# Block-sparse attention with Fourier mixing on one core: folded Fourier stage, exp in place in PSUM, two-unit slots, queues in written order

## The chip, the cores and the metric

The kernel runs on one core of a Trainium2 chip. The metric is the device time of one execution in microseconds (us), lower is better. The profile shows five queues of the core that run side by side (in the 229.0 us of batch 0's attention before, PE was busy 143.5 us, DVE 215.5, POOL 191.6 and ACT 79.6): PE (matrix products, with weight loads shown apart as PEld), DVE, ACT and POOL (element-wise work), and SP, which here only issues transfers. PEclk in the profile is the clock that was granted to PE, 1.00 being full speed; the traces record either 1.00 or 0.50 at any one time, and other values are means. All timed and profiled runs compared here were fast-state runs.

## The reference

The input is a batch of 4, with 8 heads, 768 tokens and head size 64. Attention is followed by a Fourier mixing layer and two dense layers:

```
attn = exp(scores * scale), masked by 32x32 blocks, rows normalised;   o = attn @ v
x    = o with the heads side by side                       # 4 x 768 x 512
u    = x + real(fft(fft(x, tokens), channels))
un   = (u - mean(u)) / sqrt(var(u) + 1e-6)
out  = u + relu(un @ w_ch1) @ w_ch2                        # 512 -> 2048 -> 512
```

## The kernel before

Attention works in *units*: a pair of heads, half of the queries (384 columns), 128 keys. There are 12 units in a pair of heads, 4 pairs in a batch and 192 units in all. One unit goes PE (scores), ACT (exp), DVE (mask), PE (values), while POOL adds the masked exponentials for the row sums:

```
        s = ps_s.tile([P, 2, 512], FP32, tag="s", name="s")     # PSUM, two buffers
        ... two score matmuls into s ...
        e = ep.tile([P, 2, HS], FP32, tag="e", name="e")        # SBUF
        nc.scalar.activation(out=e, in_=s[:, :, 0:HS], func=ACT.Exp, scale=scale)
        m = mask[:, c, half * HS:(half + 1) * HS].rearrange("p (o s) -> p o s", o=1)
        nc.vector.tensor_tensor(out=e, in0=e, in1=m.broadcast_to([P, 2, HS]), op=ALU.mult)
        ...
        nc.gpsimd.tensor_add(out=acc_of[n, half], in0=acc_of[n, half], in1=e)
```

The Fourier stage is done with cosine and sine tables on PE, along tokens and then across channels, using one symmetry (half the output columns). Once per pair a *turn* transposes q and k of the next pair. During batch 0 the two weight matrices are also rounded, in 16 pieces, on ACT, DVE and POOL. The main loop:

```
    for u in range(units + 9):
        if u < units:            scores(u)          # with exp, mask and sums
        if 0 <= u - 3 < units:   values(u - 3)
        ...  place, norm, mix, turn, and every third u: w_round(u // 3)
```

The order of this text is only a wish: the framework's scheduler decides how the instructions stand in each queue.

## Time and profile before

| quantity, from the trace before | value |
|---|---|
| device time, median | 1554.4 us |
| busy: PE / DVE / POOL / ACT | 1369 / 674 / 465 / 271 us |
| start of the first normalising multiply | 259.5 us |
| one later pair of heads | 34.3 us |
| Fourier stage, first normalising multiply (618.3) to first hidden matmul (678.9) | 60.6 us |
| period of a batch | 358.5 us |

PE is the busiest engine, but it isn't full everywhere: attention leaves it idle (27.7 of 34.3 us busy in a later pair) and batch 0 is filled by DVE and POOL (215.5 and 191.6 of 229.0 us). A saving on an engine therefore counts only in a stage where that engine is what the others wait for.

### The profile page before, as it was taken

The numbers are of one execution on the slowest core, as the hardware profiler recorded it, in microseconds if no ns is written. First come the engines' busy times: TensorE is split into PE (matmuls) and PEld (weight loads), VectorE is DVE, ScalarE is ACT, GpSimd is POOL, SyncE is SP. The second block draws the span as 40 slices with busy tenths as digits, with TensorE's granted clock in tenths as the row PEclk, the third lists the DMA queues.
The fourth block names the chain that finished last, engine by engine and source line by source line (L and its number), as shares of the span: only waits on it lengthen the run. The fifth ranks groups of instructions, "written<-read, shape, count | busy, mean of one in ns | idle before, by whom it ended". The sixth has DMA issues, their size and how long they took to land.

```text
span 1551.9 us, 11529 instructions
## 1 busy us (share of the span) xinstructions
PE 1369.0 (88%) x4657; PEld 678.0 (44%) x4657; DVE 673.6 (43%) x682; ACT 271.1 (17%) x383; POOL 465.1 (30%) x253
## 2 busy tenths in 40 slices
PE   6664478999999887999999888999999887999998
PEld 3111123764553222675454222485454322685453
DVE  3999997320003878240001788440000777240000
ACT  3343322100001333000000333101000323000000
POOL 2898885000002666010000666210000558010000
PEclk9777788999999998999999999999999989999999
DMA  7323210000001111000001111000000200000000
GB/s 257 102 92 118 85 29 24 0 0 7 14 7 42 33 31 31 1 0 7 14 1 41 31 35 37 0 1 0 19 2 14 53 16 1 0 1 0 21 0 22
DMA packets 63008, 46.19 MB, mean 30 GB/s; under 512 B 51404, under 2 KB 56548, under 8 KB 61668
## 3 DMA queue, kind: packets, MB, share of 16 engines
q1 hardware_dynamic: 61604, 41.97, 9.1%
q10 hardware_dynamic: 1344, 3.42, 0.6%
q8 instruction: 38, 0.62, 0.2%
q14 instruction: 22, 0.18, 0.0%
HBM read 39.08 MB, written 6.29 MB: 29 GB/s over the span
## 4 chain that ended last, share of the span: by engine, by line
issue 36%; PE 32%; DVE 25%; POOL 5%; ACT 2%; DMA 1%; SPq 0%; POOLq 0%; DVEq 0%; ACTq 0%
DVE e L269 18%; PE z L345 8%; PE pq L361 6%; PE hp L401 5%; PE y L417 5%; POOL acc L272 3%; PE s L263 2%; PE o L286 2%; DVE w_sb L218 2%; DVE wraw L216 1%; ACT e L267 1%; PE m L173 1%; PE sp L306 1%; DVE x L333 1%; DVE wraw L221 1%
## 5 line engine op out<-in xcount | busy, mean ns | idle before, releaser
L269 DVE TENSOR_TENSOR e<-e,mask 128x768 f32<-128x768 f32 x192 | 356.9, 1903 | 75.0 <-ACT e L267 75.0
L417 PE MATMUL y<-w_sb,hs 128*128 128x512 f32 x768 | 333.8, 593 | 0.0
L401 PE MATMUL hp<-unT,w_sb 128*128 128x384 f32 x1024 | 332.5, 486 | 0.0
L274 POOL TENSOR_TENSOR acc<-acc,e 128x768 f32<-128x768 f32 x128 | 290.7, 2271 | 10.4 <-DVE e L269 1.0
L263 PE MATMUL s<-qT,kT 64*128 64x384 f32 x768 | 213.6, 596 | 46.2 <-ACT e L267 46.2
L401 PEld LDWEIGHTS hp<-unT,w_sb 128*128 128x128 f32 x1024 | 194.2, 190 | 136.8 <-issue 4.8
L272 POOL TENSOR_TENSOR acc<-e 128x768 f32<-128x768 f32 x32 | 63.7, 1991 | 633.6 <-PE sp L306 632.0
L286 PE MATMUL o<-e,vr 128*64 128x384 f32 x768 | 186.6, 561 | 44.6 <-DVE e L269 41.7
L417 PEld LDWEIGHTS y<-w_sb,hs 128*128 128x128 f32 x768 | 145.1, 190 | 177.6 <-issue 172.2
L267 ACT ACTIVATE e<-s 128x768 f32<-128x768 f32 x192 | 152.0, 809 | 360.3 <-POOL acc L272 153.3
L419 DVE TENSOR_TENSOR x<-y,x 128x512 f32<-128x512 f32 x24 | 16.6, 691 | 321.3 <-PE y L417 321.3
L409 DVE TENSOR_SCALAR hs<-hp 128x768 f32<-128x768 f32 x32 | 30.6, 957 | 284.7 <-PE hp L401 284.7
L263 PEld LDWEIGHTS s<-qT,kT 64*128 64x128 f32 x768 | 69.4, 205 | 158.0 <-ACT e L267 74.0
L286 PEld LDWEIGHTS o<-e,vr 128*64 128x64 f32 x768 | 41.8, 146 | 172.1 <-DVE e L269 87.1
L407 ACT ACTIVATE hs<-hp 128x768 f32<-128x768 f32 x32 | 25.9, 810 | 444.4 <-PE hp L401 444.4
L345 PE MATMUL z<-cs_sb,x 128*128 128x385 f32 x192 | 76.1, 548 | 11.7 <-DVE x L333 11.7
L243 PE MATMUL tp<-ident,kr 128*128 128x128 f32 x96 | 21.6, 349 | 57.4 <-DVE qT L246 42.1
L374 POOL TENSOR_SCALAR rstd<-mv 128x1 f32<-128x1 f32 x24 | 5.2, 217 | 222.7 <-DVE mv L372 222.7
L345 PE MATMUL z<-sn_sb,x 128*128 128x385 f32 x192 | 64.8, 486 | 0.0
L345 PEld LDWEIGHTS z<-cs_sb,x 128*128 128x128 f32 x192 | 40.3, 215 | 45.5 <-issue 16.7
L223 POOL TENSOR_TENSOR wraw<-wraw 128x1024 f32<-128x1024 f32 x16 | 46.0, 2876 | 46.1 <-DVE wraw L221 21.6
L349 DVE COPY zs<-z 128x385 f32<-128x385 f32 x16 | 9.0, 560 | 107.6 <-ACT zc L348 107.6
(78 smaller groups left out, 832.1 us busy)
## 6 DMA issues: line engine op xcount, KB each, us to landing
wraw<-in_moe_w_ch_dram SPq DMA_DIRECT2D x16, 1024.0 KB, 5.0
qr<-in_q_dram SPq DMA_DIRECT2D x32, 192.0 KB, 3.5
kr<-in_k_dram SPq DMA_DIRECT2D x32, 192.0 KB, 3.3
vr<-in_v_dram SPq DMA_DIRECT2D x32, 192.0 KB, 2.5
out_dram<-x SPq DMA_DIRECT2D x24, 256.0 KB, 2.0
cs_sb<-in_cos_s_dram ACTq DMA_DIRECT2D x1, 1155.0 KB, 5.3
sn_sb<-in_sin_s_dram ACTq DMA_DIRECT2D x1, 1155.0 KB, 7.8
cd_sb<-in_cos_d_dram ACTq DMA_DIRECT2D x1, 514.0 KB, 5.4
```

What stands on the lines that cost most here:

```text
L218: nc.vector.scalar_tensor_tensor(out=dst.bitcast(U32), in0=hi, scalar=0x80000000, in1=a, op0=ALU.bitwise_and, op1=ALU.bitwise_or)
L223: nc.gpsimd.tensor_mul(out=a.bitcast(FP32), in0=lo.bitcast(FP32), in1=a.bitcast(FP32))
L263: nc.tensor.matmul(s[:, i, 0:HS], kT[D * i:D * i + D, c * P:(c + 1) * P], qT[D * i:D * i + D, half * HS:(half + 1) * HS], start=True, stop ...
L267: nc.scalar.activation(out=e, in_=s[:, :, 0:HS], func=ACT.Exp, scale=scale)
L269: nc.vector.tensor_tensor(out=e, in0=e, in1=m.broadcast_to([P, 2, HS]), op=ALU.mult)
L272: nc.gpsimd.tensor_add(out=acc_of[n, half], in0=e_of[u - 1], in1=e)
L274: nc.gpsimd.tensor_add(out=acc_of[n, half], in0=acc_of[n, half], in1=e)
L286: nc.tensor.matmul(o[D * i:D * i + D, :], vt[:, i, c, :], e[:, i, :], start=(c == 0), stop=(c == C - 1))
L345: nc.tensor.matmul(z[:, g, 0:KS], x[:, c, d * P:(d + 1) * P], tab[:, c, :], start=(c == 0), stop=(c == C - 1))
L361: nc.tensor.matmul(pq[:, g, 0:KD], zz[:, d, c:S:C], tab[:, d, :], start=(d == 0), stop=(d == ND - 1))
L401: nc.tensor.matmul(ps[:, j, 0:G * P], w1_sb[:, d, f * P:(f + 1) * P], unT[g][:, d, :], start=(d == 0), stop=(d == ND - 1))
L417: nc.tensor.matmul(y, hs[f // (NF // 2)][:, f % (NF // 2), o * P:(o + 1) * P], w2_sb[:, f, :], start=(f == 0), stop=(f == NF - 1))
```

## The change

The intent was threefold: less PE work in the Fourier stage (both symmetries folded away on DVE first, tokens in an order that pairs them), a cheap mask multiply, and a known order of work. Cut to its core (reordered; cuts are marked):

```
-        e = ep.tile([P, 2, HS], FP32, tag="e", name="e")
-        nc.scalar.activation(out=e, in_=s[:, :, 0:HS], func=ACT.Exp, scale=scale)
+        nc.scalar.activation(out=s[:, :, 0:HS], in_=s[:, :, 0:HS], func=ACT.Exp, scale=scale)
+        e = ep.tile([P, 2, HS], FP32, tag="e", name="e")
-        nc.vector.tensor_tensor(out=e, in0=e, in1=m.broadcast_to([P, 2, HS]), op=ALU.mult)
+        nc.vector.tensor_tensor(out=e, in0=s[:, :, 0:HS], in1=m.broadcast_to([P, 2, HS]),
+                                op=ALU.mult)
 ...
-    acc_p: 1 buffer;  ps_t: 2 (PSUM);  ps_o: 2
+    acc_p: 2 buffers; ps_t: 1 (PSUM);  ps_o: 1;  ps_m: 2, for the Fourier and dense layers
-    WN = 1024          # weight rounding in 16 pieces
+    WN = 512           # in 32 pieces
 ...
+        def fold():    # sums and differences of mirrored tokens and channels, on DVE
+            tt(out=sa, in0=xA, in1=xB, op=ALU.add)
+            tt(out=sd, in0=xA, in1=xB, op=ALU.subtract)
+            ... 14 operations; then about a quarter of the matmuls, then unfolding on DVE
 ...
+    def slot(sl):                                  # two units
+        if sl > 0 and sl <= B * SB:
+            for u in units:
+                values(u - SLOT)
+        if sl < B * SB:
+            for u, s in [(u, scores(u)) for u in units]:
+                weigh(u, s)                        # exp, mask, sums
+        ... place, row sums; at the third slot after a batch: norm, Fourier, dense layers
+        if sl % SP == 3 and sl // SP + 1 < len(pairs):
+            turn(sl // SP + 1)
+        ... v load; from slot 4 on: one table copy
+        while w_next < min(len(wchunks), 2 * sl):
+            w_round(w_next)
+            w_next += 1
+    with tc.manual_schedule():                     # queues keep the order of the text
+        for sl in range(B * SB + 6):
+            slot(sl)
```

A switch that hands out the dense layers in pieces among the attention slots is in the code, but off. Not shown: the mask's numbers go from BF16 to 8-bit integers, the Fourier tables are now put in order by copies during batch 0, and a check on the size of q and k moves from DVE to ACT, where it is part of the turn.

## The prediction

> **What bounds the kernel now.** I read the page first: its chain, then the slices.
>
> ```profile
> issue 36%; PE 32%; DVE 25%; POOL 5%; ACT 2%; DMA 1%; SPq 0%; POOLq 0%; DVEq 0%; ACTq 0%
> ...
> PE   6664478999999887999999888999999887999998
> ...
> DVE  3999997320003878240001788440000777240000
> ```
>
> No single engine bounds it. Four batches repeat one pattern: attention (DVE digits 7 to 9), the Fourier stage, then two dense matmul layers (PE 9, DVE 0). "Issue 36%" is PE streaming through those layers. So I cut the span into stages (start:end, length, busy us per engine, granted PE clock, DMA):
>
> ```profile
> 34.00:263.00 229.00, 143.49 (x549) 47.23 (x548) 215.52 (x136) 79.64 (x100) 191.55 (x75) 0.79 0.26 80
> 263.00:323.00 60.00, 59.50 (x220) 44.37 (x220) 25.09 (x57) 5.20 (x11) 4.76 (x13) 0.96 0.00 1
> 323.00:494.00 171.00, 171.00 (x485) 86.83 (x483) 15.63 (x20) 11.20 (x16) 0.00 (x0) 1.00 0.04 14
> 510.00:545.00 35.00, 27.88 (x122) 9.50 (x122) 26.73 (x20) 11.66 (x18) 22.22 (x11) 0.90 0.14 34
> ```
>
> The columns after the length are PE, PEld, DVE, ACT, POOL. Batch 0 attention also rounds the weights and is bound by DVE (94%) with POOL behind it. Fourier and dense layers are bound by PE. One later head pair takes 34.3 us (equal chain pieces start at 545.10 and 579.40) with no engine full: a round of waits. The batch period is 358.5 us (first Fourier matmul after 263.7, 622.4, 980.8). Two groups and two waits say what the round is:
>
> ```profile
> L269 DVE TENSOR_TENSOR e<-e,mask 128x768 f32<-128x768 f32 x192 | 356.9, 1903 | 75.0 <-ACT e L267 75.0
> L274 POOL TENSOR_TENSOR acc<-acc,e 128x768 f32<-128x768 f32 x128 | 290.7, 2271 | 10.4 <-DVE e L269 1.0
> ...
> POOL acc L272 <- PE sp L306: 632.0, 26, 171.3
> ...
> ACT e L267 <- POOL acc L272: 153.3, 32, 8.4
> ```
>
> The single accumulator keeps POOL waiting for PE's row sums, and exp waits for POOL to give back an e buffer. And the mask multiply is slow only beside POOL:
>
> ```profile
> 610.88 0.55 DVE L312 TENSOR_TENSOR sums<-sp,sums 128x384 f32<-128x384 f32 x1
> ...
> 613.62 4.32 DVE L269 TENSOR_TENSOR e<-e,mask 128x768 f32<-128x768 f32 x2 [1.73 <-ACT e L267]
> ...
> 624.68 1.81 DVE L269 TENSOR_TENSOR e<-e,mask 128x768 f32<-128x768 f32 x2
> ...
> 612.82 8.98 POOL L274 TENSOR_TENSOR acc<-acc,e 128x768 f32<-128x768 f32 x4
> ```
>
> POOL's adds end at 621.8. Two multiplies before that take 4.32 us, two after it 1.81. L312, whose first operand is in PSUM, takes 0.55 us although a POOL add runs from 610.93.
>
> [...] L269 (two SBUF inputs) 0.945 us alone, a median of 2.56 fully beside POOL; L312 (one) the same either way; a POOL add 1.80 alone, 2.41 beside L269. [...] the clock record drops to half for 6.8 us once per pair, hence 0.90. [...] each of these drops follows the turning of q and k.
>
> **The change, part by part.** The new program leaves its interleaving switch off, so each queue runs as written: two-unit slots (24 per batch), and at the third slot after a batch its norm, Fourier stage and dense layers, with no attention inside.
>
> *Attention slot.* From the trace: one unit's scores occupy PE 0.84 us and are complete after 0.92; exp starts 0.11 later and takes 0.81; DVE follows after 0.03; values take 0.80 and start 0.05 after the multiply. The multiply from PSUM I take as 0.96 (fit: PSUM operations of 384 and 512 elements took 0.55 and 0.69), next start 0.08 before its end. As PE is in order (values, values, scores, scores), the loop is 0.80 + 0.92 + 0.11 + 0.81 + 0.03 + 0.88 + 0.96 + 0.05 = 4.56 us per two units. POOL needs 1.67 x 1.8 = 3.0, so its waits vanish.
>
> *Turn slot, one in six.* With one transpose buffer (two before), x's transposes and four groups of q and k alternate with copies: after the second multiply (3.70) the x copy ends at 4.2, then four rounds of about 0.55 (three transposes) + 0.55 (copy) + 0.15 of hand-over, the last copy hidden: values begin at 8.2, the slot takes 9.8. PE idles or only transposes for 6 us, so the 6.8 us drop of the clock stays; values and scores at half clock took 1.48 and 1.58, twice the time, which delays the chain by some 2.8.
> Pair: 5 x 4.56 + 9.8 + 2.8 = 35.4 us against 34.3. The much cheaper multiply gains nothing here: its time comes back as exposed PE chain. Per slot 5.9.
>
> *Batch 0.* 32 half-size roundings, two in each of 16 slots. POOL: 2 x 2.9 (half of 2.88 + 2.80, plus overhead) + 1.67 x 2.1 = 9.3; DVE: 2 x 2.85 (half of 2.44 + 2.04 + 1.06, plus overhead) + 2 x 0.88 + 1 for copies and tables = 8.5. They hinder each other: 9.5 per slot. Start 35 (34.1 before) + first slot 5 + 16 x 9.5 + 9 x 5.9 + 4 = 249 at the first norm (258 before, with 56 units done instead of 54).
>
> *Fourier.* Before: norm at 618.1, first hidden matmul at 681.5: 63.4, all on PE but the first 4. PE's new work: 5,769 columns along tokens and 2,309 across; a 384-column matmul costs 0.645, so 9.7 and 3.9 us instead of 32.7 and 21.5. But DVE works alone around it. Norm: two multiplies beside POOL (1.81, 2.21) and four of 0.60 = 6.4. Fold: SBUF-SBUF at 1.04 ns per element (0.68 for 512, 0.945 for 768), 14 operations, PE released after 7.3. Along: 9.7, plus 2.5 for a cold clock. First across matmuls, copy out: 1.6. Then per 128 tokens on DVE: two of 0.46, eight of about 0.20 and two tiny ones, statistics 0.73 + 0.18, rstd wait 1.0, normalize 0.46 = 5.1; three, plus 1.1 for the odd row: 16.4. Last transposes and copy 1.2. Sum 45.1, and 2.5 for the cold start of the hidden layer: 47.6. Gain 16 per batch.
>
> *Dense layers.* Unchanged matmuls: 165.5 (last batch, 1379.4 to 1544.9) + 1.3 for transposes = 167. In the 171.3 of the earlier batches some attention and twelve transposes were tucked in; now they are exposed, and that is in the slots.
>
> *Sum.* One batch adds 47.6 + 167 = 215 to its slots. 249 + 4 x 215 + 70 remaining slots x 5.9 - 4 + 12 for the tail (three nearly empty slots, and the 7 us that lie between the last matmul and the end before) = 1530 span; the device time is 2 to 3 above that. As I counted every wait in full, I settle at 1525.
>
> **The rivals.** (a) *Attention really becomes faster*: if the clock doesn't drop and the transposes interleave better, a pair takes 31 instead of 35.4: 79 slots are 13 pairs, 57 us less, about 1468. For it: PE stays busy in 3.3 of 4.56 us; against: the drop came with every turn before. (b) *Old order was worth more*: the old schedule slipped attention into the dense layers and placed work wherever an engine was free; strictly ordered queues may add waits that I don't see (24 small q loads per pair at about 0.6 us of issue each are 14 us of 35, hidden if loaded a pair ahead). 1 us more per slot is 1600. For it: DVE, ACT and PE are now tied in one loop; against: the loads are a pair ahead. (c) *PE work sets it*: the 45 us saved per batch on PE came fully through: 4 x 45 = 180 less, 1375. Against: PE waits for fold and for across on DVE, in program order, with nothing else to do.
>
> **Range and chances.** The slot is the weight: 0.3 us on 70 slots is 21; 5 us on a Fourier stage is 20; batch 0 is sure to 12. Together about 32: 1465 to 1575 holds it 8 in 10, wider than the sum because in-order waits add up one way. The 2% line (1524) lies at my estimate: faster 0.47, same 0.43, slower 0.10.
>
> **What would show it.** Right: the multiply near 0.96 us and POOL's add near 1.8 outside batch 0; pairs of 34 to 36 us; granted clock still near 0.9 there; Fourier stage 45 to 50 us with PE busy under half of it and DVE waited for; dense layers 167. Wrong: a multiply from PSUM still over 1.3 us; a pair under 32 or over 38; DMA or SP among the long waits; batch 0's norm before 235 or after 270.

Passages that no trace of this case shows are cut from the paragraph on the mask multiply and the clock, and a clause from the expectation of experiment 12; the cuts are marked. The sum came to a span of 1530 us, from which the prediction settled at 1525. What it says of the clock and of PE's order, with the numbers beside it:

- Half clock: in the later batches of the kernel before, in each of the eight turns with a stretch of 4.6 us in which PE idles or only transposes, a drop of 6.8 us begins within that stretch; the three turns tucked into the dense layers (longest such stretch 0.7 us) show none, so of these eleven "every turn" holds for the eight alone. That the drop stays in the new turn slot is inferred from this.
- The two terms of 2.5 us, for a cold clock and a cold start, are estimates. The trace before has a drop of 6.8 us at the Fourier stage of batch 1, from 619.6 to 626.4, while the first matmul there starts at 620.3; at the start of the hidden layer it shows none (clock 1.00 from 626.4 on), so the second term is borne out only by the trace after. In the changed kernel's batch 0 the clock is at half from 284.4 to 298.1 and from 311.7 to 332.2 (first Fourier matmul 294.6, first hidden one 326.7), so 3.5 and 5.5 us of that follow a start; half of it is 1.7 and 2.7 us.
- 0.645 us for a matmul of 384 columns: such a one stands as two records in the trace before, and those of the hidden layer start 0.323 us apart (median).
- "PE is in order": the trace of the changed kernel shows a slot's eight value records from 566.67 and its eight score records from 568.33, in the written order.

## The result and the profile after

The changed kernel takes 1558.7 us (median of four runs, 1557.5 to 1560.4), the kernel before 1554.4 (1551.3 to 1555.6). The ratio is 1.0032, with a 95% interval of 1.0014 to 1.0050: the same within 2%, and certainly no gain. Ratios here are the mean time of one kernel's fast runs over that of the other's fast runs of the same rounds, so they are not quite the ratio of the medians.

From the page of the changed kernel, slices of PE and DVE, and the chain that ended last:

```profile
PE   6554457579998777579999777579999767679997
...
DVE  1796974530001333541011333631010343440000
...
PE 65%; DVE 19%; POOL 5%; issue 4%; ACT 4%; SPq 2%; DMA 1%; DVEq 0%; POOLq 0%; ACTq 0%
```

In the later attention stretches DVE's digits have gone from 7 and 8 to 3 and 4: the saving on DVE is real. PE's digits there are 7 instead of 8. The share "issue" (36% before) has become PE's own work in the dense layers and waits in between. The stages of the changed kernel, with columns as in the prediction (batch 0's attention, its Fourier stage, its dense layers, one later pair):

```profile
34.00:281.70 247.70, 135.38 (x531) 50.23 (x529) 180.81 (x215) 92.91 (x153) 169.30 (x108) 0.75 0.30 88
281.70:326.60 44.90, 22.12 (x84) 13.88 (x84) 27.78 (x69) 6.37 (x17) 5.56 (x8) 0.68 0.00 1
326.60:495.80 169.20, 169.08 (x460) 87.55 (x460) 16.37 (x30) 9.68 (x20) 2.33 (x6) 0.98 0.03 8
555.60:590.70 35.10, 25.75 (x126) 9.76 (x124) 13.44 (x17) 12.58 (x20) 18.04 (x11) 0.90 0.14 34
```

The Fourier stage went from 60.8 (in batch 0, 259.4 to 320.2) to 44.9 us, but the pair still takes 35.1 us although DVE needs 13.4 us in it instead of 26.7. Batch 0 went the wrong way, and DVE and POOL are less full there than before. The groups and waits that answer to those before:

```profile
L426 POOL TENSOR_TENSOR acc<-acc,e 128x768 f32<-128x768 f32 x128 | 235.8, 1842 | 143.9 <-DVE e L420 136.8
L420 DVE TENSOR_TENSOR e<-s,mask 128x768 f32<-128x768 f32 x192 | 175.4, 951 | 251.4 <-ACT s L417 248.4
```

```profile
POOL acc L424 <- DVE e L420: 506.7, 14, 153.5
...
DVE e L420 <- ACT s L417: 248.4, 82, 10.7
...
PE o L438 <- DVE e L420: 136.8, 81, 12.2
...
POOL acc L424 <- PE sp L467: 72.0, 15, 5.0
```

The multiply fell from 1.903 to 0.951 us and the add from 2.271 to 1.842. Exp's wait for POOL (153.3 us before) is gone from the list of waits. POOL's wait for the row sums fell from 632 to 72 us by these lists, but most of that is a change of label: before, three waits of 171.3 us in it span a Fourier stage and the dense layers, when POOL has no adds to do, and after, three like them (153.5 us each) are put down to DVE's multiply. Within one later pair POOL's wait for the row sums fell from 12.0 to 4.8 us. What is left in attention is a ring: DVE waits for ACT (248 us), PE's values wait for DVE (137 us). The timeline of one quiet stretch shows how it turns:

```profile
566.67 1.73 PE L438 MATMUL o<-e,vr 128*64 128x384 f32 x8 [1.31 <-DVE e L420]
...
568.33 1.56 PE L409 MATMUL s<-qT,kT 64*128 64x384 f32 x8
...
569.29 1.50 ACT L417 ACTIVATE s<-s 128x768 f32<-128x768 f32 x2 [0.31 <-PE s L409]
...
570.19 1.82 DVE L420 TENSOR_TENSOR e<-s,mask 128x768 f32<-128x768 f32 x2 [2.71 <-ACT s L417]
```

The number after the start time is the duration; the bracket holds the idle time before it and what ended it. Values, scores, exp and multiply follow one after another, and each engine waits for the others' part.

Slot by slot (from the start of a slot's first exp to that of the next slot's), the trace gives 4.5 us for a quiet slot and a mean of 12.5 us for a slot with a turn. In batch 0, slots 1 to 16 carry the roundings: the three with a turn (3, 9, 15) last 17.4, 17.6 and 18.0 us, and the other 13 a mean of 9.8. The timeline of slot 9 in batch 0:

```profile
125.20 3.75 POOL L426 TENSOR_TENSOR acc<-acc,e 128x768 f32<-128x768 f32 x2
...
127.21 2.03 DVE L361 TENSOR_SCALAR wraw<-wraw 128x512 uint32<-128x512 uint32 x1
...
130.34 0.42 DVE L361 TENSOR_SCALAR wraw<-wraw 128x512 uint32<-128x512 uint32 x1
...
137.05 0.56 DVE L390 COPY qT<-tp 128x384 f32<-128x384 f32 x1 [0.99 <-PE tp L387]
137.67 0.97 PE L387 MATMUL tp<-ident,qr 128*128 128x128 f32 x3 [0.65 <-DVE qT L390]
...
140.77 0.90 PE L387 MATMUL tp<-ident,kr 128*128 128x128 f32 x3 [0.65 <-DVE kT L390]
...
142.91 0.65 ACT L357 ACTIVATE wraw<-wraw 128x512 f32<-128x512 uint32 x1
...
145.89 1.35 POOL L368 TENSOR_TENSOR wraw<-wraw 128x512 f32<-128x512 f32 x1 [7.50 <-ACT wraw L360]
```

Two things are to be seen. The same rounding step (L361) takes 0.42 us when POOL is idle at its start, and 2.03 us when POOL's adds run beside it: they end at 128.95, it ends at 129.24. Of the 32 such steps, 21 take 0.41 to 0.43 us; the other 11, all begun while POOL was at work, take 0.69 to 2.03. And from 137 to 142 us the turn holds the queues: transposes and copies alternate, ACT begins the slot's roundings only at 142.91, behind the turn in its queue, and POOL is without work for 7.5 us.

### The profile page after: what moved, and what is told of

Its sections match the earlier page's. It is cut to its first block, busy times and chain, and to the rows that moved or that the text cites. A ratio compares the mean times of both kernels' runs of the same rounds, so it can differ in the third digit from the quotient of the medians.

```text
span 1558.6 us, 11612 instructions
## 1 busy us (share of the span) xinstructions
PE 1221.0 (78%) x4165; PEld 578.4 (37%) x4165; DVE 520.5 (33%) x840; ACT 309.0 (20%) x535; POOL 401.6 (26%) x285
## 4 chain that ended last, share of the span: by engine, by line
PE 65%; DVE 19%; POOL 5%; issue 4%; ACT 4%; SPq 2%; DMA 1%; DVEq 0%; POOLq 0%; ACTq 0%
PE hp L651 22%; PE y L666 21%; PE o L438 8%; DVE e L420 6%; PE s L409 5%; POOL acc L426 4%; PE tp L387 3%; ACT s L417 3%; DVE w_sb L363 3%; PE zp L542 2%; DVE x L488 1%; DVE wraw L361 1%; DVE x L600 1%; PE zp L553 1%; PE m L271 1%
## 5 line engine op out<-in xcount | busy, mean ns | idle before, releaser
L426 POOL TENSOR_TENSOR acc<-acc,e 128x768 f32<-128x768 f32 x128 | 235.8, 1842 | 143.9 <-DVE e L420 136.8
L420 DVE TENSOR_TENSOR e<-s,mask 128x768 f32<-128x768 f32 x192 | 175.4, 951 | 251.4 <-ACT s L417 248.4
L417 ACT ACTIVATE s<-s 128x768 f32<-128x768 f32 x192 | 145.0, 793 | 206.0 <-PE s L409 205.4
L409 PE MATMUL s<-qT,kT 64*128 64x384 f32 x768 | 168.2, 561 | 0.0
L657 DVE TENSOR_SCALAR hs<-hp 128x384 f32<-128x384 f32 x64 | 35.7, 558 | 292.2 <-PE hp L651 292.2
L655 ACT ACTIVATE hs<-hp 128x384 f32<-128x384 f32 x64 | 31.4, 491 | 434.5 <-PE hp L651 434.5
L387 PE MATMUL tp<-ident,qr 128*128 128x128 f32 x96 | 28.4, 397 | 70.6 <-DVE x L457 47.8
L542 PE MATMUL zp<-cs_sb,sa 128*128 128x385 f32 (+1 forms) x48 | 24.4, 643 | 55.9 <-DVE sa L518 55.9
L368 POOL TENSOR_TENSOR wraw<-wraw 128x512 f32<-128x512 f32 x32 | 43.2, 1348 | 35.2 <-ACT wraw L360 21.6
L641 PE MATMUL utp<-ident,un 128*128 128x128 f32 x96 | 20.2, 350 | 36.7 <-DVE un L618 24.6
L363 DVE SCALAR_TENSOR_TENSOR w_sb<-wraw 128x512 uint32<-128x512 uint32 x32 | 46.5, 1454 | 1.1
```

Source lines behind the costliest of these rows:

```text
L363: nc.vector.scalar_tensor_tensor(out=dst.bitcast(U32), in0=hi, scalar=0x80000000, in1=a, op0=ALU.bitwise_and, op1=ALU.bitwise_or)
L368: nc.gpsimd.tensor_mul(out=a.bitcast(FP32), in0=lo.bitcast(FP32), in1=a.bitcast(FP32))
L387: nc.tensor.transpose(tp[:, c * P:(c + 1) * P], t[:, T * half + c, :, :], ident)
L409: nc.tensor.matmul(s[:, i, 0:HS], kT[D * i:D * i + D, c * P:(c + 1) * P], qT[D * i:D * i + D, half * HS:(half + 1) * HS], start=True, stop ...
L417: nc.scalar.activation(out=s[:, :, 0:HS], in_=s[:, :, 0:HS], func=ACT.Exp, scale=scale)
L420: nc.vector.tensor_tensor(out=e, in0=s[:, :, 0:HS], in1=m.broadcast_to([P, 2, HS]), op=ALU.mult)
```

## The experiments

In all of them "time" is the median of four runs, and each ratio is to the kernel before in the same rounds (its medians there were 1551.5 to 1555.6). The pair times and slot lengths are taken from the starts of exp in the trace. Batch 0 is given as the time at which the first normalising multiply comes up ("first norm": before 259.4, changed 281.7; the multiply's own record starts 0.1 to 0.2 us later in every run). Where a sum of experiments is compared, the changed kernel's own slots are the base: quiet 4.5, turn 12.5 us.

### 1. Scores ahead of values

```
         if sl > 0 and sl <= B * SB:
-            for u in units: values(u - SLOT)           # moved
         if sl < B * SB:
             for u, s in [(u, scores(u)) for u in units]:
                 weigh(u, s)
+        if sl > 0 and sl <= B * SB:
+            for u in units: values(u - SLOT)
```

> In each slot the next two scores are issued ahead of the two values; nothing else moves. Theory (the in-order PE queue stretches the attention loop by putting 0.80 us of values between a multiply and the scores that refill its PSUM buffer): a quiet slot falls from 4.53 to 3.3-3.7 us, where PE alone (2 x 0.84 + 2 x 0.80 = 3.3) bounds it, and about 70 slots give 60 to 80 us: 1475 to 1500 us. Rival 1 (DVE or ACT, not the order, holds the loop): slot stays 4.4-4.6, total 1550 to 1562. Rival 2 (the loop shortens, but turn slots, which hold the waits, take it back): quiet slot 3.5, total 1520 to 1545.

Measured: 1475.8 us, ratio 0.951. A quiet slot takes a mean of 3.6 us, a turn slot 10.4, a pair 27.7. The theory holds, with the slot in its range and the total at the good end. A different order of two parts of a slot is worth 83 us (1558.7 - 1475.8), because in the written order values stood between a multiply and the scores that refill the PSUM buffer just freed (in the changed kernel's quiet stretch above, 1.66 us from the start of the values, 566.67, to that of the scores, 568.33).

### 2. A second transpose buffer

```
-                tp = ps_t.tile([P, HS], FP32, tag="t", name="tp")
+                tp = (ps_t.tile([P, HS], FP32, tag="t", name="tp") if half == 0 else
+                      ps_m.tile([P, HS], FP32, tag="m", name="tp"))
```

> The second half of each turn takes its transpose buffer from the two-buffer pool, so that transposes and copies overlap. Theory (the one transpose buffer stretches the turn slots): a turn slot falls from about 12.4 us by 1.5 to 3, 16 of them: 1510 to 1535 us. Rival (the turn slot is held by the clock drop and by DVE's and ACT's queue order, not by the buffer): under 0.5 us per turn slot, 1550 to 1560.

Measured: 1503.6 us, ratio 0.969, more than expected. A turn slot takes a mean of 8.4 us instead of 12.5; quiet slots are unchanged. The window of one pair (same columns) shows why it is more:

```profile
536.60:567.00 30.40, 22.85 (x126) 8.80 (x124) 13.44 (x17) 12.47 (x20) 18.10 (x11) 1.00 0.15 39
```

The granted clock is 1.00 in this pair instead of 0.90. The same twelve transposes are there, and the longest time that PE idles in a turn is 2.2 us in both. But the stretch of a turn without any matmul other than transposes falls from between 7.6 and 8.1 us to between 4.7 and 5.7. Of the eleven later turns, five show no drop to half clock and six a drop of 3.4 us; in the changed kernel all eleven show one, of 6.8 or 10.2 us. In this kernel the one buffer cost both its waits and the clock.

### 3. The kernel before with exp in place alone

```
-        nc.scalar.activation(out=e, in_=s[:, :, 0:HS], func=ACT.Exp, scale=scale)
+        nc.scalar.activation(out=s[:, :, 0:HS], in_=s[:, :, 0:HS], func=ACT.Exp, scale=scale)
-        nc.vector.tensor_tensor(out=e, in0=e, in1=m.broadcast_to([P, 2, HS]), op=ALU.mult)
+        nc.vector.tensor_tensor(out=e, in0=s[:, :, 0:HS], in1=m.broadcast_to([P, 2, HS]),
+                                op=ALU.mult)
```

> The kernel before with one part of the change alone: exp in place in PSUM and the mask multiply reading it there. Theory (the cheap multiply is worth much in an order that can use it; the new order is what gave it back): multiply 0.95 us instead of 1.90, POOL's add 1.8 instead of 2.27, batch 0 (DVE-bound) 40 us shorter, other pairs 34.3 to 29-32: 1460 to 1500 us. Rival (the PSUM buffer, held until the multiply has read it, stops the scores in the old order too): pair 34 or more, and only batch 0 gains: 1520 to 1550. Second rival: slower than before, over 1570.

Measured: 1451.2 us, ratio 0.935. A pair takes 26.6 us instead of 34.3, and the first norm comes at 219.7 instead of 259.4. The theory holds in kind; the total came out below its range (1460 to 1500), with a pair shorter than the 29 to 32 expected. The multiply takes 0.954 us here with the mask still in BF16, so the mask's new type is not what made it cheap:

```profile
489.70:516.30 26.60, 24.65 (x124) 8.78 (x122) 16.07 (x21) 11.38 (x16) 18.10 (x10) 1.00 0.18 45
```

PE is busy 24.65 of 26.6 us: with the multiply out of the way, PE becomes the bound of attention.

### 4. The changed kernel without written order

```
-    with tc.manual_schedule():
+    with nullcontext():
```

> The changed kernel with the queues left to the scheduler of the kernel before instead of being kept in written order. Theory (written order puts waits into attention and into batch 0 that the scheduler would fill): batch 0 shorter by 15 to 30 us and the turn slots by 1 to 3 each: 1490 to 1535 us. Rival (the waits come from buffers, not from order): 1545 to 1570. Second rival: the scheduler puts work ahead of the chain of the Fourier stage: over 1580.

Measured: 1388.7 us, ratio 0.894, far below the theory's 1490 to 1535: right in kind, but a gain of 170 us on the changed kernel where at most 69 were expected. The first norm is at 242.4 (39 us earlier), a pair takes 26.3 us. Nothing was taken out of the program; only the places in the queues differ:

```profile
490.00:516.30 26.30, 25.18 (x124) 8.54 (x122) 13.98 (x17) 12.86 (x20) 18.01 (x11) 1.00 0.18 45
```

The next lines, from the timeline of the same pair, show where its turn went:

```profile
505.22 0.55 PE L387 MATMUL tp<-ident,qr 128*128 128x128 f32 x3
505.70 0.87 PE L438 MATMUL o<-e,vr 128*64 128x384 f32 x4
506.49 0.91 PE L409 MATMUL s<-qT,kT 64*128 64x384 f32 x2
507.33 0.55 PE L387 MATMUL tp<-ident,qr 128*128 128x128 f32 x3
```

Between two groups of transposes stand one unit's values and some scores, so the copy of the one transpose buffer is hidden. Elsewhere scores and values alternate unit by unit (x4, x4), where the written order has values of two units and then scores of two (x8, x8).

### 5. Three places mended by hand

Edits 1 and 2 together, with edit 6 below, still in written order.

> Written order kept, with three of its places mended by hand: scores ahead of values, a second transpose buffer, and the weight roundings ahead of the turn in each slot. Theory (these places are nearly the whole price of the written order, and each takes away a different wait): swap alone gave a pair of 27.8 us and the second buffer a pair of 30.5 instead of 35; together, at full clock, 25 to 27, and batch 0 first norm 265 instead of 282: 1385 to 1430 us. Rival (the two shorten the same wait, so they don't add): pair 27.5 or more, 1450 to 1475.

Measured: 1426.2 us, ratio 0.918, at the upper end of the theory's range. A quiet slot takes 3.4 us, a turn slot 7.8, a pair 24.6 us, less than the scheduler's 26.3. The first norm, at 256.3, is later than the scheduler's 242.4. So inside a plain pair two local places were the price of the written order. The hand-made order stays 37.5 us behind the scheduler's (1426.2 - 1388.7) for two other reasons: batch 0, 13.9 us, and the pairs into which a Fourier stage and the dense layers fall, 242 us against 232.

### 6. Roundings ahead of the turn

```
+        while w_next < ...:  w_round(w_next) ...       # moved up
         if sl % SP == 3 and sl // SP + 1 < len(pairs):
             turn(...)
         ...
-        while w_next < ...:  w_round(w_next) ...
```

> The changed kernel with one move: in each slot the weight roundings are issued ahead of the turn. Theory (in batch 0 the turn's chain of transposes and copies, queued ahead of the roundings on DVE and ACT, keeps POOL and DVE idle for 6 to 20 us in each of three turn slots): 12 to 25 us less, all before the first norm: 1533 to 1547 us. Rival (the turn slot's time is only moved to the next slot, as DVE's own work fills batch 0): 1555 to 1563. Nothing after batch 0 changes in either case.

Measured: 1562.7 us, ratio 1.006: a miss, the rival is right. The turn slots of batch 0 grew to 22.6, 23.1 and 25.6 us, and the slot after each fell from 8.6 to 9.0 us to 4.5. Changing which of the two stands first only moves the time from one slot to the next; both have to be carried either way.

### 7. Table copies on ACT

```
-                nc.vector.tensor_copy(out=dst..., in_=...)      # nine places
+                nc.scalar.copy(out=dst..., in_=...)
```

> The changed kernel with the copies that unfold the Fourier tables on ACT instead of DVE. Theory (they were under-estimated in batch 0: 3.2 us on DVE in one slot instead of 1.2): with ACT taking them, 8 to 18 us less before the first norm: 1541 to 1551 us. Rival (ACT's copies then stand in front of exp in its queue, or DVE wasn't what the slots wait for): 1556 to 1575.

Measured: 1556.4 us, ratio 1.001, against 1558.7 for the changed kernel in its own rounds: at the edge of the rival's range. The first norm is 4.8 us earlier, the total by 2 to 3. The table copies are at most a small part of the cause.

### 8. The dense layers handed out, in the scheduler's order

```
-INTERLEAVE = False
+INTERLEAVE = True
-    with tc.manual_schedule():
+    with nullcontext():
```

> The changed kernel with the scheduler's order instead of written order, and its own switch for handing out the Fourier stage and the dense layers in pieces among the attention slots of the next batch turned on. Theory (DVE, POOL and PE have their work at different times; with attention beside the dense layers PE is busy nearly always outside batch 0 and its 1220 us of work become the bound): 1290 to 1350 us, PE over 90% busy. Rival (the shared PSUM buffers and the transposes tie the two together, or the slots get DVE work of the Fourier stage ahead of their multiplies): 1370 to 1420. Third: worse than both kernels, as the pieces delay the chain of attention.

Measured: 1346.4 us, ratio 0.867, at the end of the theory's range; PE is busy 89% of the span. The switch alone, in written order, could not be run: its build stops because the queues would wait for each other in a circle.

### 9. Exp to SBUF again, in written order

```
-        nc.scalar.activation(out=s[:, :, 0:HS], in_=s[:, :, 0:HS], func=ACT.Exp, scale=scale)
+        nc.scalar.activation(out=e, in_=s[:, :, 0:HS], func=ACT.Exp, scale=scale)
-        nc.vector.tensor_tensor(out=e, in0=s[:, :, 0:HS], in1=m...
+        nc.vector.tensor_tensor(out=e, in0=e, in1=m...
```

> The changed kernel in its written order, with exp going to SBUF again and the mask multiply reading two SBUF operands. It tests the sentence of the prediction that the cheaper multiply gains nothing in the written order. Theory (in that order every microsecond of the multiply lies on the PE-ACT-DVE chain, so a dear multiply is paid twice per slot and again where POOL runs beside it): quiet slot 6 to 7.5 us instead of 4.53, multiply 1.9 to 2.4 us, POOL's add over 2.1: 1650 to 1750 us. Rival (the chain hides it): slot under 5, below 1590.

Measured: 1646.5 us, ratio 1.060, just below the theory's range. Multiply 1.33 us, POOL's add 2.05, quiet slot 5.6, so less than expected in each; the pair takes 41.1 us. The sentence under test falls: in the written order, too, exp in place with its cheap multiply is worth 88 us (1646.5 - 1558.7).

### 10. Exp to SBUF again, in the scheduler's order

Edits 4 and 9 together.

> The changed kernel in the scheduler's order, with exp going to SBUF again: of the change, the Fourier folding, the token order, the two-unit loop and the two accumulators remain. Theory (parts add up: in place was worth 102 us in the kernel before, and the rest 1451 - 1389 = 62): 1480 to 1505 us, pairs of 33 to 35 us again. Rival (two accumulators already cure the waits of the old pair, so that in place is worth little beside them): pair under 30, 1400 to 1440.

Measured: 1463.8 us, ratio 0.943, between theory and rival: pairs of 29.7 to 30.5 us, multiply 1.59. So the other parts cure some of the old pair's waits, and the parts don't simply add: folding and the rest are worth 91 us without exp in place (1554.4 - 1463.8), and 62.5 with it (1451.2 - 1388.7).

### 11. Small mends on top of 8

Edits 2 and 7, and half of the Fourier additions moved into a wait for the deviation.

> The version with scheduler's order and handed-out dense layers (1346 us), with a second transpose buffer, the table copies on ACT, and the second half of the Fourier additions put into the wait for the reciprocal deviation. Theory (small waits left on DVE in batch 0 and in Fourier): 1325 to 1342. Rival (the scheduler already fills these places; the extra use of the shared PSUM pool costs what the rest gains): 1343 to 1360.

Measured: 1350.4 us, ratio 0.870 beside 0.867 for 8, with overlapping intervals. The rival is right: the scheduler had filled these places.

### 12. Half the roundings moved out of batch 0, on top of 8

```
-        t = big.tile([P, 3 * WN], U32, tag="big", name="wraw")       # of six buffers
+        t = wr_p.tile([P, 3 * WN], U32, tag="wr", name="wraw")       # one; big: five
...
+                if b == 0 and half == 0:       # beside each hidden-layer piece of batch 0
+                    rest.append((0.0, lambda: w_next < len(wchunks) and w_step()))
```

> The version with scheduler's order and handed-out dense layers (1346 us), with the rounding of the second weight matrix taken out of batch 0's attention and put between the hidden-layer pieces of batch 0, where DVE and POOL have little to do (one rounding buffer of its own, five of the six big buffers). Theory (batch 0 is bound by DVE and POOL[...]: 16 roundings of 2.8 us of POOL and 1.5 of DVE less): the first norm 35 to 60 us earlier, of which some comes back in batch 1: 1295 to 1325. Rival (batch 0 is bound by the chain of scores, exp, multiply, values, not by the roundings): norm under 20 us earlier, 1335 to 1350. Third: the single rounding buffer or five big buffers stall the layers: over 1350.

Measured: 1378.9 us, ratio 0.889, worse than 8; the third outcome, and in batch 0 the rival was right (first norm 219.5 against 238.1 in 8, 19 us, where the theory had 35 to 60). ACT waited 126.2 us in total for the loads of the weights, as there was only one rounding buffer (the loads, in lines not shown, also went from four pieces ahead to one); a build with two beside the five big ones is refused for lack of space (one pool asks for 6 KB per partition where 3.66 are left). Whether the move would pay with more space stays open.

### 13. No turns in batch 0

```
         raw = loaded.pop(n)
+        if 0 < n < NP:
+            turned[n] = turned[n - 1]      # wrong on purpose
+            return
```

> The changed kernel in its written order without the turns of pairs 1 to 3: batch 0 uses pair 0's turned q and k for all its pairs, so its result is wrong on purpose. Theory (a turn adds its own serial time to a slot full of roundings): the three turn slots of batch 0 fall from 17.4-18.0 us to 9.5-10.5, the first norm from 282 to 256-261, total 1533 to 1540 us. Rival 1 (the turn was hidden under the roundings, as predicted, and the roundings are dear): slots stay over 16, total 1553 or more. Rival 2 (turn and roundings hinder each other): falls by over 10 us per slot, total under 1527.

Measured: 1540.2 us, ratio 0.991 (result wrong). The same slot, first with its turn in the changed kernel and then without it:

```profile
127.60:145.20 17.60, 8.40 (x35) 3.74 (x33) 10.98 (x18) 6.31 (x12) 8.61 (x6) 0.61 0.07 21
```

```profile
120.30:132.10 11.80, 5.52 (x23) 2.10 (x21) 11.63 (x16) 3.73 (x6) 8.88 (x6) 0.77 0.27 73
```

DVE and POOL do nearly the same work in both, in 17.6 and in 11.8 us. The three slots fall by 6.8, 5.8 and 6.0 us, and the first norm comes at 262.0, 19.7 us earlier. The theory holds in kind, at the upper edge of its range for the total (1533 to 1540) and 1 us beyond it for the first norm; the slots, 10.7 to 12.0 us, are up to 1.5 longer than it said. So about 6.2 of a turn's 8.0 us are added to a slot of roundings, and the rest is hidden.

### 14. No roundings

```
-            w_round(w_next)
+            wraw.pop(w_next)               # loaded, not rounded: wrong on purpose
```

> The changed kernel in its written order without the weight roundings: the weights are loaded into their buffers but not rounded, and a constant is put in their place late in batch 0, so the result is wrong on purpose. Theory (turn and roundings simply add): turn slots of batch 0 at 12 to 13.5 us as in later batches, other slots 4.5 to 6 (with table copies), first norm near 185 to 195 instead of 282; the roundings' price is then about 90 us for 16 slots, 5.6 per slot. Rival (they hinder each other): turn slots at 12.5 but the roundings' price in turn slots differs from that in the others by more than 2 us. The total, 1460 to 1475, says little more.

Measured: 1487.4 us, ratio 0.957 (result wrong). Turn slots of batch 0: 12.1, 14.1 and 13.3 us. The first norm is at 209.2, later than expected (185 to 195); two quiet slots of 11.0 and 12.3 us, beside loads (DMA share 1.00 from 75 to 95 us and 0.90 from 115 to 135), are part of this and come of the experiment. By this run the roundings cost 72.5 us (281.7 - 209.2), 4.5 per slot of the 16. The price in a turn slot, 4.5 us on average (17.7 - 13.2), is much the same as in the others (9.8 - 5.6 = 4.2; without the two slots beside the loads, 5.3), so turn and roundings nearly add, as the theory said.

### 15. Scores ahead of values, on top of 8

Edits 1 and 8 together.

> The version with scheduler's order and handed-out dense layers (1346 us), with scores issued ahead of values. Theory (the scheduler already puts scores where they are ready): within 6 us of 1346. Rival (the written priority still matters): 1325 to 1338.

Measured: 1334.4 us, ratio 0.859. The rival is right: even the scheduler's order depends on the order of the text. This is the best version found, 14% faster than both kernels, and its result is correct.

## Why the prediction was right or wrong

The change does what it should: the first table below shows it faster by 166 us in the scheduler's order. It came out even with the kernel before because the written order takes back 170.

| median time, us | old Fourier stage and loop, scheduler's order | new, scheduler's order | new, written order |
|---|---|---|---|
| exp to SBUF | 1554.4 | 1463.8 | 1646.5 |
| exp in place in PSUM | 1451.2 | 1388.7 | 1558.7 |

The prediction forecast 1525 from a sum of 1530. With the 2 to 3 us that it names for the device time, the sum is 1532 to 1533; the step down to 1525, because "every wait" had been counted, was a guess in the wrong direction. Set against the trace, the terms are:

| term | predicted | measured |
|---|---|---|
| start to first norm (batch 0) | 249 | 281.7 |
| four times Fourier and dense layers | 860 | 855.6 |
| attention slots after that (70 at 5.9, less 4) | 409 | 409.6 |
| tail | 12 | 11.7 |
| sum | 1530 | 1558.6 |

**Attention slot and turn slot: right.** 4.56 us predicted and 4.5 measured; 12.6 with the clock's loss and 12.5 measured; the pair 35.4 and 35.1. The multiply at 0.96 and the add at 1.8 came as predicted, and so did the drop of the clock (0.90 in the pair); how the turn slot splits into waits and clock was not measured apart. POOL's waits for the row sums shrank rather than vanished, and the 632 us that the prediction shows for them are mostly (3 x 171.3) time in which POOL has no adds to do.

**Fourier and dense layers: right.** 47.6 predicted and 43.0 to 46.2 measured, with PE busy 22.1 of 44.9 us in batch 0, under half as predicted; 167 predicted and 168 to 170 measured. The 63.4 that the prediction gives for the stage before is 3 us too long: the first hidden matmul of batch 1 is at 678.9, not 681.5; and the dense layers from there to their last matmul took 167.9, not 171.3. Neither figure was used in the sum.

**Batch 0: wrong, and this is the step that failed: "9.5 per slot", taken for all "16 x 9.5".** It came from the engines' loads in a slot of roundings, and counted the three slots with a turn like any other, as though the turn were hidden beneath the roundings. In the changed kernel the 13 slots without a turn measured 9.8. The turn slots measured 17.4 to 18.0, together 24.5 us over the prediction. Without the turns in batch 0 (experiment 13) the first norm came 19.7 us earlier, so the turns explain 60% of the 32.7 us that were missed. Nearly all of the other 13.0 is the term's size: with the turns taken out, the 16 slots still took 162.9 us instead of 152, and the first slot took 6.3 instead of 5, together 12.2. The roundings' price in batch 0, 16 x (9.5 - 5.9) = 58 us by the prediction, was 72.5 by experiment 14. One reason is seen in the timeline, where a rounding step of 0.42 us lasts 2.03 beside POOL's adds. The prediction averaged this from the kernel before. In that timeline the step ends 0.29 us after POOL's second add; whether it waited for that add, and whether such waits are the whole of the remaining 13 us, is not shown. My first explanations were tried: order within the slot fell (6), and table copies gave at most 4.8 us (7). "Batch 0 is sure to 12" was too sure.

**"Its time comes back as exposed PE chain": half right.** The chain is real and the numbers of the slot are right, but "gains nothing here" is wrong: against the same order with the costly multiply it gains 88 us (9). What stands against it is the order itself, which costs 183 us with exp in SBUF and 170 with exp in place. I took the order as given, and so read its price as the multiply's failure. The trace shows where it is paid: in the changed kernel scores whose PSUM buffer is free stand behind two units of values (the multiply that frees the first buffer ends at 566.61, the values start at 566.67 and the scores at 568.33), and exchanging them (1) takes 83 us away.

**The rivals.** (a), a pair of 31 us if the clock stays up, is what a second transpose buffer makes of the kernel: 30.4 us at clock 1.00 (2). It did not come by itself. (b), that the old order was worth more, is right in substance, by 170 us, though not as the longer slots that it forecast: the slots came as predicted, and the price was already inside them. Its suspected cause, the issue of loads, appears in no long wait. (c), PE as the bound, is not this kernel, but it is close in version 15, where PE is busy 88% of the span. The 45 us per batch that (c) takes off PE do not follow from the prediction's own figures (32.7 + 21.5 - 9.7 - 3.9 = 40.6); PE's busy time fell by 37 (1369.0 to 1221.0 over four batches).

## What to carry to other kernels

When a change removes time from an engine and fixes the order of the queues too, measure the two apart: here one line, the scheduler taken out, was worth more than all the rest (170 us against 166). In a queue of fixed order put the work that starts the next chain (here scores) ahead of the work that only ends the last one (here values; 83 us in experiment 1), and give a chain of alternating engines two buffers (turn slot 8.4 us instead of 12.5 in experiment 2) or other work in between (as the scheduler does in experiment 4, whose whole order makes the pair 26.3 us instead of 35.1). When adding up a stage, ask of each serial chain in it whether another engine's load truly covers it; if both sit in the same queues of written order, add them, as here 6.2 of a turn's 8.0 us came on top of the roundings (experiment 13).

## What these traces show of the hardware

- DVE beside POOL in a profile: the slower DVE instruction is shown as busy all the while (2.03 us beside POOL's adds for a step that takes 0.42 alone). In batch 0 of the changed kernel both engines are shown as busy in 137 of 248 us; how much of that is such slowing was not measured.
- Transposes and the clock: the clock drops at every later turn of the changed kernel, where PE idles 2.2 us at most, but does nothing other than idle and transpose for 7.6 to 8.1 us. With the same twelve transposes among other matmuls (experiment 4, no such stretch in a turn) it stays 1.00 in the pair shown. Stretches of 4.6 us in the kernel before brought a drop each time, those of 4.7 to 5.7 in experiment 2 in six of eleven turns. How long a stretch may be is not shown beyond that. The drops lasted 6.8 us per pair before, 6.8 or 10.2 after and 3.4 in experiment 2.
- Where exp goes: an exp of 128x768 took 0.793 us into PSUM and 0.809 into SBUF, so 2%; the gain of exp in place came from DVE's multiply (0.951 instead of 1.33 to 1.90 us).
- A multiply whose first operand is in PSUM took 0.952 us on average both beside POOL's work and alone, where two SBUF operands took 0.95 alone and a median of 2.56 beside it.
